# Moved keys copied once by ScalarE before the state increments read them, in a linear-attention and feed-forward kernel

## The chip, the cores and the metric

The kernel runs on 1 core of one Trainium2 chip. The metric is the device time of one execution in microseconds (us), and lower is better. TensorE (PE in the profile, with its weight loads as PEld) multiplies matrices, VectorE (DVE) and ScalarE (ACT) work elementwise, GpSimd (POOL) and SyncE (SP) here mostly issue DMA transfers. Each engine runs its own list of instructions in order.

## The reference, cut to what matters

```python
# q, k, v, f_logit: (B=4, H=8, S=768, D=48)
f = 1 / (1 + exp(-f_logit))
for t in range(S):
    state = f[:, :, t, :, None] * state + einsum('bhd,bhe->bhde', k[:, :, t], v[:, :, t])
    y[:, :, t] = einsum('bhd,bhde->bhe', q[:, :, t], state)
x = y.transpose(0, 2, 1, 3).reshape(B * S, H * D)      # 3072 x 384
h = x @ w_in                                           # 384 -> 2048
out = (max(h, 0) + alpha * min(h, 0)) @ w_out          # 2048 -> 384
```

The first half is a gated linear recurrence: a 48x48 state for each head decays by f and takes in the product of key and value. The second half is a feed-forward network with a leaky Relu. Everything is float32.

## The kernel before, in words

**Tiling.** The sequence is cut into 6 chunks of 128 positions and the batch into 2 pairs, which makes 12 steps, numbered 0 to 11 here; steps 0 and 1 are the first chunk (c = 0) of the two pairs. Inside a step all positions of a chunk are worked on at once by matrix products, and the state is carried to the next chunk of the same pair, in `vs[bp]`.

**Pieces and the hand-written order.** A step is a set of generators, each cut by `yield` into pieces. The letters in the lists START and USUAL (lines 31 to 40) call them: P `prepare` (loads, gates, decays, on ACT and DVE), K `keys_moved`, O `carry`, S and T `scores` of the two batch rows, Y `attend`, n `network` (of the step before, in the loop). `flat` writes the order out; every engine but POOL takes its instructions in exactly this order. Steps up to 4 are ordered by START, steps from 5 on by USUAL, which is repeated. A "+" there means a piece of the next step, so that the keys of step n are moved at the end of round n-1.

**How the keys travel.** The last part of `prepare` computes the decayed keys `ks`; line 415 transposes them in blocks of 32 on DVE into `kt`. `keys_moved` (lines 457 to 466) then puts the blocks in place with 16 DMAs from `kt` into `ksn`: 8 on SP's queue and 8 on POOL's. The third piece of `carry` reads them: line 532 multiplies keys and values to the state increments in the PSUM banks `pd`. Ahead of it, for every step with c > 0, line 525 issues two very small matmuls (64x64 by 64x4), one for each half of the partitions. Their result is never used: they read one column of each moved block, so that PE's waits for the 16 transfers stand on them. In steps 0 and 1 there is no transfer; there ACT copies transposed keys from PSUM (line 518). The fourth piece of `carry`, `moved(0)` (lines 542 to 546, DVE), adds the increments to the decayed state, and `attend` (line 623) needs it for the second half of the chunk. `moved(1)` follows in the last piece of `attend`.

**What stands around it.** From step 4 on PE does line 497 (products of the chunk's two halves, 32 records) just before line 525, and goes on with the network after line 532. ACT does the Relu of the network (`neg`, line 673), copies A (453, 504, 612), `us` (334) and `y` (630). `y` and `ksn` are the same buffer (one tag, one buffer). The network writes `ph` (line 668) into 4 PSUM banks in turn; a bank is free again when ACT has made `neg` and DVE both halves of `gate` (line 675, two instructions) of it. `neg` has two buffers, and after every fourth bank DVE makes four sums (line 754). The products `pa` to `pe` (line 707) use the same four banks.

Of the kernel before, what the change touches and what calls it, by code (L numbers as in the profile page):

```python
# [21 lines left out]
U = 2  # L22
# [16 lines left out]
)  # L39
USUAL = "S:2 T:2 n:3 P+ n S P+ T S n:3 T n Y n O P+ O P+ O Y n O P+ Y:2 n:2 P+:2 K+ n P+"  # L40

LOOSE = ("a", "w", "b", "g", "W", "i", "X")

def flat(start, usual, steps=12):
    out = []
    for word in start.split():
        key, _, times = word.partition(":")
        out += [(key,) if key in LOOSE else (key[0], int(key[1:]))] * int(times or 1)
    for n in range(BEGUN, steps + 1):
        for word in usual.split():  # L50
            key, _, times = word.partition(":")
            m = n + key.count("+") - (key == "n")
            if m < steps:
                out += [(key[0], m)] * int(times or 1)
    return out

ORDER = flat(START, USUAL)


@with_exitstack  # L60
def kernel(
# [30 lines left out]
    nc = tc.nc  # L92
# [3 lines left out]
    D = DM // H  # L96
# [3 lines left out]
    T = U * C  # L100
    W = U * HP * C
# [70 lines left out]
    for m in range(1, NB):  # L172
        lo = UO[m] + (4 if m == 1 else 0)
        n = NB - m
# [4 lines left out]
    for half in range(2):  # L179
        for m in range(1, NQ):  # L180
            n = NQ - m
# [9 lines left out]
    ident = const.tile([128, 128], F32, tag="ident", name="ident")  # L191
# [65 lines left out]
    def rows(par):  # L257
        return slice(64 * par, 64 * par + D)
# [4 lines left out]
    def halves(cc):  # L263

        return slice(CH * cc, CH * cc + CH), slice(CH * (1 - cc), CH * (1 - cc) + D)
# [191 lines left out]
    def keys_moved(bp, c, x):  # L457
# [7 lines left out]
                    in_=kt[32 * a:32 * (a + 1)].rearrange("p (g b x) -> p g b x", b=NJ, x=32)[:, :, b, 0:n])  # L465
        yield

    def carry(bp, c, x):

        i = f"{bp}_{c}"  # L470
        home = more if (bp, c) == steps[0] else pairs
        off = home[0]
        if not c:
            half = home[1]
            for u in range(U):
                for hp in range(HP):
                    for j in range(NJ):
                        g = (u * HP + hp) * NJ + j
                        o = (u * HP + hp) * 16
                        for par in range(2):  # L480
                            r_ = rows(par)
                            nc.tensor.matmul(half[DB * j:DB * (j + 1), par, o:o + 16], lhsT=x["k16"][r_, g],
                                             rhs=x["q16"][r_, g], start=True, stop=True)
            yield
            for u in range(U):
                o = u * HP * 16
                nc.scalar.copy(ad[:, u, :, :, 16:DB], half[:, :, o:o + HP * 16].rearrange("p r (h t) -> p r h t", h=HP))  # L487
            yield
        q3, ks, kh, f64 = (x[n] for n in ("q3", "ks", "kh", "f64"))
        for u in range(U):  # L490
            for hp in range(HP):
                a = (u * HP + hp) * NC2
                h_ = slice(64 * (hp % 2), 64 * (hp % 2) + 2 * DB)
                o = (u * HP + hp) // 2 * 2 * DB
                for par in range(2):
                    r_ = rows(par)
                    nc.tensor.matmul(off[h_, par, o:o + 2 * DB], lhsT=kh[r_, a:a + 2].rearrange("p c s -> p (c s)"),  # L497
                                     rhs=q3[r_, a:a + 2, 2], start=True, stop=True)
        yield
        for cc in range(NC2):  # L500
            s_ = slice(CH * cc, CH * cc + DB)
            for e in range(2):
                of = off[64 * e + DB * cc:64 * e + DB * (cc + 1), :, 0:U * HP * DB]
                nc.scalar.copy(A[s_].rearrange("p u (r h e) t -> p r u h e t", r=2, e=2)[:, :, :, :, e, CH * cc + DB:CH * (cc + 1)],
                               of.rearrange("p r (u h c t) -> p r u h c t", u=U, h=HP // 2, c=NC2)[:, :, :, :, cc])


        if not c:
            yield
            pk = home[1]  # L510
            for u in range(U):
                for hp in range(HP):
                    a = (u * HP + hp) * NC2
                    nc.tensor.transpose(pk[:, u, hp * 128:(hp + 1) * 128], ks[:, a:a + 2].rearrange("p c s t -> p (c s t)"), ident)
            yield
            ksn = x["ksn"] = work.tile([128, U, HP * 128], F32, tag="ksn", name=f"ksn_{i}", bufs=1)
            for u in range(U):
                nc.scalar.copy(ksn[:, u], pk[:, u])
        yield
        pd = home[1]  # L520
        ksn = x["ksn"]
        if c:
            for par in range(2):
                r_ = slice(64 * par, 64 * par + 64)
                nc.tensor.matmul(pd[r_, par, 508:512], lhsT=ident[r_, r_], rhs=ksn[r_, 0, 0:128:32], start=True, stop=True)  # L525
        for u in range(U):
            for hp in range(HP):
                for cc in range(NC2):
                    for par in range(2):
                        o = (u * HP + hp) * D  # L530
                        s_ = halves(cc)[0]
                        nc.tensor.matmul(pd[rows(par), cc, o:o + D],  # L532
                                         lhsT=ksn[s_, u, hp * 128 + 64 * par:hp * 128 + 64 * par + D],
                                         rhs=vs[bp][s_, cc, u, (2 * hp + par) * D:(2 * hp + par + 1) * D], start=True, stop=True)

        def moved(cc):

            of, to = halves(cc)[1], halves(1 - cc)[1]
            was, then = (vs[bp][p, a, :, 0:DM].rearrange("p u (h e) -> p u h e", e=D)
                         for p, a in ((of, cc), (to, 1 - cc)))  # L540
            if c or cc:
                nc.vector.tensor_tensor(then, was, f64[of].unsqueeze(3).broadcast_to((D, U, H, D)), ALU.mult)
            for par in range(2):
                now = pd[rows(par), cc, 0:U * HP * D].rearrange("p (u h e) -> p u h e", u=U, e=D)
                if c or cc:
                    nc.vector.tensor_tensor(then[:, :, par:H:2], then[:, :, par:H:2], now, ALU.add)
                else:
                    nc.scalar.copy(then[:, :, par:H:2], now)

        x["moved"] = moved  # L550
        yield
        moved(0)
        yield
# [236 lines left out]
    with tc.manual_schedule(engines={mybir.EngineType.PE, mybir.EngineType.DVE, mybir.EngineType.Activation,  # L790
                                     mybir.EngineType.SP}):
        run = {}
        for n, step in enumerate(steps):
            x = {}
            for key, stage_ in zip("POYKn", (prepare, carry, attend, keys_moved, network)):
                run[key, n] = stage_(*step, x)
            run["S", n], run["T", n] = (scores(u, *step, x) for u in range(U))
        for key in ORDER:
            next(run[key] if key in run else pieces[key[0]])
# [55 lines left out]
```

## Time and profile before

| | us |
|---|---|
| three runs | 610.0, 608.13, 609.3 |
| median | 609.3 |
| the profiled execution: its time | 608.89 |
| the profiled execution: its span, first to last instruction | 607.1 |
| granted TensorE clock, mean | 0.994 |

The span is what the profile's rows add up to; 1.8 us of the execution's time lie around it. PE is the busiest engine, DVE comes next. In the rows, a float32 matmul of the program is two records of PE (32 matmuls of line 532 are 64 records), "idle before" is the time in which the engine did nothing just before a row, with what ended it, and EVENT_SEMAPHORE is an instruction of an engine's queue that only waits.

### The profile page before, as it was taken

How to read it: one execution, taken by the hardware profiler on the slowest of the kernel's cores; microseconds unless marked ns; L12 is line 12 of the kernel's file. 1: busy time of each engine (PE TensorE's matmuls, PEld its weight loads, DVE VectorE, ACT ScalarE, POOL GpSimd, SP SyncE). 2: the span in 40 equal slices, each digit the busy share in tenths (PEclk: the TensorE clock that was granted, in tenths of full speed). 3: DMA queues.
4: the chain of work that ended last, by engine and by line, in shares of the span. 5: the costliest groups of instructions: out<-in, count | busy, mean ns of one | idle time of the engine just before them, and what ended most of it. 6: DMA issues, size and time to landing. Idle time of an engine off the chain costs nothing.

```text
span 607.1 us, 18178 instructions
## 1 busy us (share of the span) xinstructions
PE 583.9 (96%) x7786; PEld 521.8 (86%) x7786; DVE 495.0 (82%) x998; ACT 242.3 (40%) x419; POOL 85.4 (14%) x162
## 2 busy tenths in 40 slices
PE   4679999999999999999999999999999999999997
PEld 2568767899899899899899899899889899899997
DVE  7889999998997788598888988988988986982351
ACT  4579944424513712341550541542433424322110
POOL 9210014023003003003001201200300300300000
PEclk9979999999999999999999999999999999999999
DMA  8949516123033111402501601601601601201000
GB/s 269 312 148 350 186 37 141 36 77 92 11 94 99 19 27 36 149 2 56 155 2 46 165 3 42 169 3 41 171 1 39 170 4 29 53 2 24 30 1 26
DMA packets 52880, 50.36 MB, mean 83 GB/s; under 512 B 26720, under 2 KB 43360, under 8 KB 52800
## 3 DMA queue, kind: packets, MB, share of 16 engines
q1 hardware_dynamic: 42784, 37.46, 21.2%
q0 software_dynamic: 5504, 9.90, 6.4%
q10 hardware_dynamic: 4512, 1.85, 1.3%
q8 instruction: 61, 1.00, 0.7%
q14 instruction: 19, 0.16, 0.1%
HBM read 36.21 MB, written 4.72 MB: 67 GB/s over the span
## 4 chain that ended last, share of the span: by engine, by line
PE 92%; ACT 1%; issue 1%; DMA 1%; SPq 0%; DVE 0%; ACTq 0%; DVEq 0%
PE ph L668 42%; PE pa L707 10%; PE pc L707 9%; PE pair L569 6%; PE pe L707 5%; PE pd L707 4%; PE pb L707 4%; PE pair L623 4%; PE po L688 3%; PE pair L532 1%; PE pair L497 1%; DMA xT<-y 1%; PE pair L525 1%; PE xt L642 0%; ACT us L334 0%
## 5 line engine op out<-in xcount | busy, mean ns | idle before, releaser
L668 PE MATMUL ph<-xT,w_in_sb 128*128 128x256 f32 x1152 | 255.7, 381 | 0.0
L668 PEld LDWEIGHTS ph<-xT,w_in_sb 128*128 128x128 f32 x1152 | 216.7, 190 | 31.5 <-issue 1.4
L675 DVE SCALAR_TENSOR_TENSOR gate<-neg,om,ph 128x256 f32<-128x256 f32 x192 | 81.9, 479 | 40.0 <-ACT neg L673 39.8
L673 ACT ACTIVATE neg<-ph 128x512 f32<-128x512 f32 x96 | 56.3, 595 | 115.6 <-PE ph L668 76.9
L707 PE MATMUL pa<-w_out_sb,gate 128*128 128x192 f32 x352 | 61.9, 329 | 0.0
L707 PE MATMUL pc<-t,S 128*128 128x192 f32 x352 | 61.6, 328 | 0.0
L707 PEld LDWEIGHTS pa<-w_out_sb,gate 128*128 128x128 f32 x352 | 57.5, 190 | 1.3
L707 PEld LDWEIGHTS pc<-t,S 128*128 128x128 f32 x352 | 57.4, 190 | 0.4
L453 ACT COPY A<-q 48x512 f32<-48x512 f32 x44 | 27.1, 616 | 74.8 <-DVE q L401 74.4
L463 POOL DMA_DIRECT2D ksn<-kt x80 | 46.2, 586 | 73.2 <-DVE kt L415 46.6
L653 POOL DMA_DIRECT2D xT<-y x22 | 11.9, 545 | 302.5 <-ACT y L630 302.4
L588 DVE COPY_PREDICATED ad<-mquad,pair 128x224 f32<-128x224 int32 (+6 forms) x140 | 41.7, 298 | 5.8 <-PE pair L569 1.7
L578 DVE COPY_PREDICATED ad<-mraw,pair 128x256 f32<-128x256 int32 (+1 forms) x96 | 41.1, 452 | 4.3 <-ACT ad L487 1.3
L711 DVE SCALAR_TENSOR_TENSOR Csum<-pc,Csum 128x192 f32<-128x192 f32 x22 | 7.8, 356 | 39.9 <-PE pc L707 39.8
L357 DVE TENSOR_TENSOR us<-us,fs 128x768 f32<-128x768 f32 (+5 forms) x60 | 36.9, 615 | 1.1
L612 ACT COPY A<-ad 32x512 f32<-32x512 f32 x48 | 29.5, 615 | 20.4 <-DVE ad L588 19.8
L754 DVE TENSOR_TENSOR S<-gate 128x512 f32<-128x512 f32 x44 | 30.3, 688 | 0.8
L707 PE MATMUL pe<-w_out_sb,S 128*128 128x192 f32 x176 | 30.5, 327 | 0.0
L707 PE MATMUL pb<-t,gate 128*128 128x192 f32 x176 | 30.4, 326 | 0.0
L707 PE MATMUL pd<-w_out_sb,S 128*128 128x192 f32 x176 | 30.4, 326 | 0.0
L630 ACT COPY y<-pair 128x512 f32<-128x512 f32 x22 | 11.8, 589 | 46.4 <-PE pair L623 45.8
L707 PEld LDWEIGHTS pe<-w_out_sb,S 128*128 128x128 f32 x176 | 28.9, 190 | 0.1
(121 smaller groups left out, 740.6 us busy)
## 6 DMA issues: line engine op xcount, KB each, us to landing
w_out_raw<-in_w_out SPq DMA_DIRECT2D x8, 767.8 KB, 7.2
w_in_raw<-in_w_in SPq DMA_DIRECT2D x8, 767.2 KB, 10.4
out<-o SPq DMA_DIRECT2D x23, 192.0 KB, 2.0
q<-in_qT SPq DMA_DIRECT2D x8, 512.0 KB, 4.7
k<-in_kT SPq DMA_DIRECT2D x8, 512.0 KB, 5.9
f<-in_fT SPq DMA_DIRECT2D x7, 512.0 KB, 3.9
vs<-in_v SPq DMA_DIRECT2D x16, 192.0 KB, 6.4
ksn<-kt SPq DMA_DIRECT2D x80, 32.0 KB, 2.1
```

The lines of the kernel that those rows point to most:

```text
L357: nc.vector.tensor_tensor(us[:, :, UO[m]:UO[m] + 4 * n].rearrange("p g (i r) -> p g i r", r=4), us[:, :, skip:skip + 4 * n].rearrange("p g ...
L453: nc.scalar.copy(A[halves(cc)[1], :, par * HP:(par + 1) * HP, CH * cc:CH * (cc + 1)], q3[rows(par)].rearrange("p (u h c) s t -> p u h c (s ...
L463: (nc.gpsimd if a % 2 else nc.sync).dma_start(out=ksn[32 * b:32 * (b + 1)].rearrange("p u (h x) -> p (u h) x", h=HP)[:, :, 32 * a:32 * a + n],
L569: nc.tensor.matmul(to[DB * j:DB * (j + 1), par, hp * step + lo:hp * step + hi], lhsT=keys[r_, g * DB:(g + 1) * DB], rhs=by[r_, g, lo:hi], ...
L578: nc.vector.copy_predicated(adu[:, :, :, d:4], mraw[:, d, :, d:4].bitcast(I32).unsqueeze(1).broadcast_to((128, H, NB, n)), rv[:, :, QO[d]: ...
L588: nc.vector.copy_predicated(ad[:, u, :, :, 4 * m:DB], mquad[:, lo:lo + n].bitcast(I32).unsqueeze(1).unsqueeze(1).broadcast_to((128, 2, HP, ...
L612: nc.scalar.copy(A[s_].rearrange("p u h t -> p (u h) t")[:, :, s_], ad[s_].rearrange("p u r h t -> p (u r h) t"))
L668: nc.tensor.matmul(ph[:, j * T:(j + 1) * T], lhsT=w_in_sb[:, kt, m * 128:(m + 1) * 128], rhs=xT[:, kt], start=(kt == 0 and j == 0), stop=( ...
L673: nc.scalar.activation(neg, phv, AF.Relu, scale=-1.0)
L675: nc.vector.scalar_tensor_tensor(gate[:, m % NH, m // NH], neg[:, j], om[:, m:m + 1], phv[:, j], ALU.mult, ALU.add)
L707: nc.tensor.matmul(to[:, 0:DH], lhsT=of(f), rhs=by(f), start=(f == 0 and not more), stop=(f == NH - 1), skip_group_check=True)
L754: nc.vector.tensor_tensor(to, x_, y_, op)
```

## The change

A new generator, `landed` (letter M), copies the moved keys with ScalarE from `ksn` back into the buffer `kt` from which they were moved, 48 of every 64 columns, in one instruction of 128 partitions by 768 elements. The state increments of line 532 read this copy. The two small matmuls of line 525 are gone. M stands once in every step from 2 on: in START after the ninth network piece of step 1, the one with `pa` and `pb` (M2), and directly behind K3 and K4, and in USUAL at the head of the round. The order of everything else stays.

```diff
-O2:2 P3:2 n1 ... n2 K3 Y3 n2:3 O3 P4 O3 ... n3:3 K4 Y4 O4:3 P5:2
+M2 O2:2 P3:2 n1 ... n2 K3 M3 Y3 n2:3 O3 P4 O3 ... n3:3 K4 M4 Y4 O4:3 P5:2
...
-USUAL = "S:2 T:2 n:3 P+ n S P+ T S n:3 T n Y n O P+ O P+ O Y n O P+ Y:2 n:2 P+:2 K+ n P+"
+USUAL = "M S:2 T:2 n:3 P+ n S P+ T S n:3 T n Y n O P+ O P+ O Y n O P+ Y:2 n:2 P+:2 K+ n P+"
...
+    def landed(bp, c, x):
+        parts = "p u (g x) -> p (u g) x"
+        kn = x["kt"].rearrange("p (u y) -> p u y", u=U)
+        nc.scalar.copy(kn.rearrange(parts, x=64)[:, :, 0:D], x["ksn"].rearrange(parts, x=64)[:, :, 0:D])
+        x["ksn"] = kn
+        yield
...
         ksn = x["ksn"]
-        if c:
-            for par in range(2):
-                r_ = slice(64 * par, 64 * par + 64)
-                nc.tensor.matmul(pd[r_, par, 508:512], lhsT=ident[r_, r_], rhs=ksn[r_, 0, 0:128:32], start=True, stop=True)
         for u in range(U):
...
-            for key, stage_ in zip("POYKn", (prepare, carry, attend, keys_moved, network)):
+            for key, stage_ in zip("POYKMn", (prepare, carry, attend, keys_moved, landed, network)):
```

8 rows, old and new, of the table START are left out of this document.

## The prediction

> **What bounds the kernel now.** The page's busy times and the shares of its chain that ended last come first, then the chain in order of time.
>
> ```profile
> PE 583.9 (96%) x7786; PEld 521.8 (86%) x7786; DVE 495.0 (82%) x998; ACT 242.3 (40%) x419; POOL 85.4 (14%) x162
> ...
> PE 92%; ACT 1%; issue 1%; DMA 1%; SPq 0%; DVE 0%; ACTq 0%; DVEq 0%
> ```
>
> PE sets the end. What leaves PE's list, or makes PE wait, moves the time one for one; ACT has room on the average, so only the places matter where it is late. The guards of line 525 are looked at in the view of that line and in the chain (start, length, what).
>
> ```profile
> L525 PEldq EVENT_SEMAPHORE  x79: 51/51/51, 123.3 to 548.3; - x79
> ...
> 75.40 0.84 PE pair L569 x60
> 76.25 0.86 PE pair L532 x64
> ...
> 123.75 2.60 PE pb L707 x16
> ...
> 127.32 2.80 PE pc L707 x16
> ...
> 264.62 0.62 PE pair L497 x32
> ...
> 266.64 2.80 PE pc L707 x16
> ...
> 547.45 0.62 PE pair L497 x32
> 548.24 0.21 issue
> 548.63 0.81 PE pair L532 x62
> 549.45 2.80 PE pc L707 x16
> ```
>
> In step 1, without guards, line 532 follows its forerunner without a gap (75.40+0.84 = 76.24) and takes 0.86. In step 11 the stretch from line 497 to `pc` takes 549.45-547.45 = 2.00, where 0.62+0.86 = 1.48 is work: the guards cost 0.52. In step 5 it is 2.02, so 0.54; the rounds between repeat this. The guards' own matmuls are the smaller part: eight waits a step (79 in ten steps) of 51 ns are 0.41. In step 2 a long product stands ahead of the guards instead of line 497, and there 127.32-(123.75+2.60) = 0.97 is only 0.11 over 0.86: the waits ran beside the product.
>
> The Trainium skill ("TensorE: Matmul & The Clock Gate", section "Wait — 56ns, not 53.3ns?") states that small matmuls start no closer than about 25 ns apart. By that floor two guards are worth an estimated 0.05 a step and 0.5 in ten. By it the sum below would be +1.2+0.55-0.5 = +1.25 in place of -1.9. Step 2's 0.11 is near the floor, step 11's 0.52 is not, so the measured gap decides.
>
> **The change part by part.**
>
> *What goes.* Twenty guard matmuls and PE's 80 waits. In rounds 5 to 11 the copy is ready long before its reader (in round 5 at 245.5, worked out below, with line 497 at 264.62), and PE has by then waited for later work of ACT, so nothing replaces them: 7 x 0.52 = 3.6. In steps 2 and 3, 0.1 each.
>
> But DVE must follow. `attend` needs `moved(0)`, and DVE gets there behind `pc`:
>
> ```profile
> 493.26 0.87 DVE L675 SCALAR_TENSOR_TENSOR gate<-neg,om,ph 128x256 f32<-128x256 f32 x2 [1.77 <-ACT neg L673]
> ...
> 505.23 0.36 DVE L711 SCALAR_TENSOR_TENSOR Csum<-pc,Csum 128x192 f32<-128x192 f32 x1 [0.52 <-PE pc L707]
> ...
> 506.59 1.11 DVE L546 TENSOR_TENSOR vs<-vs,pair 48x384 f32<-48x384 f32 x2
> ...
> 507.65 2.17 PE L623 MATMUL pair<-A,vs 128*64 128x64 f32 x64
> ```
>
> `moved(0)` ends at 507.70 just as line 623 starts. DVE's only idle time between the gate at 493.26 and there is 0.52. It covers 0.52 of saving, no more; any lateness of DVE in this stretch is lost from the saving.
>
> *What comes.* One ACT copy of 768 elements a step, ten in all. No row has this size, so it is bounded:
>
> ```profile
> L630 ACT COPY y<-pair x22: 586/588/593, 89.7 to 557.5; 128x512 f32<-128x512 f32 x22
> L630 ACTq EVENT_SEMAPHORE  x77: 17/38/6253, 38.6 to 549.1; - x77
> ...
> 485.15 1.05 ACT L296 COPY qd<-q 128x1024 f32<-128x1024 f32 x1
> ```
>
> It lies between 0.59 and 1.05; I take the middle, 0.82. Sixteen waits come with it, but `y` stood behind the same sixteen (some eight instructions a step, 38 ns each), so they move from line 630 to the copy. After the last landing up to 0.5 of them can remain; I take 0.3.
>
> *Queues.* The copy waits for all 16 landings, and each Relu or copy behind it on ACT waits with it. SP and POOL issue the moves when the transpose is done, as before; the buffer `ksn` is free earlier, but the transpose is what they wait for. The next transpose into `kt` must now follow line 532, which DVE's `moved(0)` does already.
>
> *Rounds 6 to 11.* Rows of SP with the landing, of ACT and of DVE:
>
> ```profile
> L463 SPq DMA_DIRECT2D ksn<-kt x8: 606/612/884, 472.3 to 477.2; - x8
> ...
> DMA to landing us min/median/max: 1.8/2.0/2.5
> ...
> 476.76 2.50 ACT L453 COPY A<-q 48x512 f32<-48x512 f32 x4 [9.98 <-DVE q L401]
> 479.17 1.07 ACT L673 ACTIVATE neg<-ph 128x512 f32<-128x512 f32 x2
> ...
> 480.75 2.52 DVE L675 SCALAR_TENSOR_TENSOR gate<-neg,om,ph 128x256 f32<-128x256 f32 x6
> ```
>
> The last keys land at 477.2+2.0 = 479.2 to 479.7, when ACT has just ended line 453. The copy then runs from about 479.5 to 480.3 and the first `neg` ends at 480.9, not 479.8. DVE is busy until 480.75, so it is 0.2 to 0.8 late, and the 1.77 idle before 493.26 takes that up before the stretch that counts. Cost nothing; without this cover up to 0.8 a round.
>
> *Round 5* has the keys later:
>
> ```profile
> L463 SPq DMA_DIRECT2D ksn<-kt x8: 602/610/618, 237.9 to 242.4; - x8
> ...
> 248.79 10.63 PE L668 MATMUL ph<-xT,w_in_sb 128*128 128x256 f32 x48
> ```
>
> Landed at 244.4, copied by 245.5, first `neg` 246.1, first pair of gates 247.0. PE needs that bank at 248.79, a margin of 1.8. Cost nothing.
>
> *Step 4* puts the copy right before its reader. ACT first has a Relu:
>
> ```profile
> 204.71 0.60 ACT L673 ACTIVATE neg<-ph 128x512 f32<-128x512 f32 x1 [2.04 <-PE ph L668]
> ...
> 206.54 8.04 PE L668 MATMUL ph<-xT,w_in_sb 128*128 128x256 f32 x36
> ```
>
> The keys have landed. The copy runs from 205.31 to 206.13, line 532 can start at about 206.2 and ends at 207.1, where the network now goes on at 206.54: +0.55 (0.3 to 0.8 by the copy's bounds).
>
> *Step 3* puts it in the way of the Relus:
>
> ```profile
> L463 SPq DMA_DIRECT2D ksn<-kt x8: 586/610/1687, 147.1 to 153.1; - x8
> ...
> 153.81 1.24 ACT L612 COPY A<-ad 32x512 f32<-32x512 f32 x2
> ...
> 155.43 2.53 DVE L675 SCALAR_TENSOR_TENSOR gate<-neg,om,ph 128x256 f32<-128x256 f32 x6
> ...
> 177.56 0.36 DVE L711 SCALAR_TENSOR_TENSOR Csum<-pc,Csum 128x192 f32<-128x192 f32 x1 [0.65 <-PE pc L707]
> ...
> 178.92 1.12 DVE L546 TENSOR_TENSOR vs<-vs,pair 48x384 f32<-48x384 f32 x2
> ...
> 180.09 1.59 PE L569 MATMUL pair<-qd,k 48*32 48x80 f32 x128
> ```
>
> ACT would come to the copy at 153.8, but the last keys land at 153.1+2.0 = 155.1. With 0.3 of waits it runs from 155.4 to 156.2; line 612 ends at 157.5, the next `neg` at 158.1. The second of the three gate pairs at 155.43 would have run at 156.3: DVE is 1.8 late. From there to 177.56 I find no idle time in DVE's timeline; then 0.65 is taken up, and `moved(1)` ends not at 180.04 but 1.2 later. Line 569 writes the banks that it reads and starts 0.05 behind it: +1.2 for PE (0.9 to 1.6).
>
> *Sum.* -0.1 (step 2) +1.2 (step 3, whose own 0.1 is lost in the wait) +0.55 (step 4) -3.6 (rounds 5 to 11) = -1.9. Against the profiled execution's 608.89 that is 607.0. The median is 0.4 above that execution, so 607.4 on its scale.
>
> **The rivals.**
>
> *Step 3 costs nothing*, because the gates or `moved(1)` have slack that the timeline hides. For it: PE's product `pd` ends at about 180.04 too, so DVE need not have been the bound. Against: DVE's row is the later by its 0.05. Sum -0.1-0.1+0.55-3.6 = -3.2, so 606.1.
>
> *DVE takes the gain back* at `attend`: the 0.52 of cover and the 0.52 of saving are equal, and a copy late by one more us in rounds 5 to 10 could leave DVE late at 493.26. If half the saving goes in seven rounds, the sum is -0.1, so 609.2. Against: the 1.77 of idle time stands in between.
>
> *The gap stays, and the kernel is slower.* If the 0.5 is not the waits of the guards but what line 532 pays wherever it follows line 497's short matmuls, with the waits merely lying in it, rounds 5 to 11 save nothing and the two early costs remain: -0.1+1.2+0.55 = +1.65, so 611.0, and up to +2.3 with both at their upper ends. It decides at a leftover gap of 0.28 a round: above that the sum is positive. Against: the row of 76.25, and eight waits of 51 ns that fill 0.41 of the 0.52. This is also the case in which the change doesn't do what it says, freeing PE of the landings.
>
> **How the numbers follow.** Forecast 0.58 (own range 606.8 to 608.0, from steps 3 and 4 at their ends), step 3 free 0.16, DVE takes back 0.12, gap stays 0.14. The range goes from the second case with step 4 at +0.3 and rounds of 0.54 (605.6) to the third with step 4 at +0.8 (609.4); it leaves out the last. A measurement here tells about 0.3%, or 1.8 us, from no change. The forecast's -1.9 lies at that edge: half of it and the second case are faster, 0.45; the other half, the third case and half of the last are same, 0.48; the rest is slower, 0.07.
>
> **What would show it.** Right: no waits of PE at line 532 in rounds 5 to 11, and 1.48 from line 497 to `pc`; idle time of PE ahead of line 532 in step 4 (about 1.0, on the ACT copy) and ahead of line 569 in step 3 (1.2, on DVE line 546, by its new number); the new copy at 0.82. Wrong: idle time of PE at line 623 on DVE, or at line 668 on gates, in every round, or a copy near or above 1.05.

## The result and the profile after

| | before | changed |
|---|---|---|
| median of 20 runs, us | 610.08 | 606.54 |
| lowest to highest, us | 608.13 to 612.76 | 604.76 to 608.97 |
| ratio of the times, 95% interval | | 0.9944 (0.9930 to 0.9958) |
| profiled execution, us | 608.89 | 607.96 |
| its span, us | 607.1 | 606.2 |

The changed kernel is 3.4 us faster (2.6 to 4.3 by the interval). Behind the new generator its line numbers are higher: 497 is now 504, 532 is 535, 546 is 549, 569 is 572, 623 is 626, 673 and 675 are 676 and 678, 707 is 710.

The page first: busy time of the engines, and the shares of the chain.

```profile
PE 580.8 (96%) x7746; PEld 518.5 (86%) x7746; DVE 495.4 (82%) x998; ACT 248.5 (41%) x429; POOL 81.7 (13%) x162
...
PE 87%; DVE 5%; ACT 1%; DMA 1%; issue 1%; ACTq 0%; DVEq 0%
```

PE has 40 records less, the guards, and ACT ten instructions more, the copies. DVE's 5% of the chain are new (before it had 0%): somewhere PE now waits for it.

The chain in order of time (start, length, what), in step 2 and in round 10, answers to the guards' rows:

```profile
125.11 2.60 PE pb L710 x16
127.70 0.86 PE pair L535 x64
128.57 2.80 PE pc L710 x16
...
500.63 0.62 PE pair L504 x32
501.26 0.72 PE pair L535 x64
501.98 2.80 PE pc L710 x16
```

From line 504 to `pc` the stretch is 501.98-500.63 = 1.35, where it was 2.00. In step 2 the increments follow `pb` directly.

Next the rows of the copy itself, and the waits of PE's queue that are left at the increments:

```profile
L471 ACT COPY kt<-ksn x10: 831/832/834, 125.7 to 526.7; 128x768 f32<-128x768 f32 x10
...
L535 PEldq EVENT_SEMAPHORE  x4: 51/51/51, 27.1 to 207.4; - x4
```

Ten copies of 0.83 each; the last wait at line 535 is at 207.4, in step 4. None is left in rounds 5 to 11.

What was paid is read by stages. This view gives the start and end of each stage, its length, the busy time (and instructions) of PE, PEld, DVE, ACT and POOL in it, then granted clock, DMA share and GB/s. The cuts are the starts of the scores of step 2, step 4 and step 5 and of the last `pe`; the first fence is the kernel before, the second the changed one.

```profile
114.18:180.09 65.91, 65.86 (x850) 60.41 (x849) 61.45 (x120) 23.17 (x41) 9.41 (x16) 1.00 0.20 51
180.09:234.92 54.83, 54.63 (x677) 50.65 (x677) 45.15 (x92) 18.16 (x32) 9.64 (x17) 1.00 0.22 57
234.92:601.11 366.19, 364.68 (x4590) 334.90 (x4590) 283.08 (x593) 123.55 (x220) 35.98 (x64) 1.00 0.22 58
```

```profile
115.53:182.71 67.18, 66.19 (x842) 60.15 (x841) 61.88 (x121) 24.50 (x43) 9.38 (x16) 1.00 0.24 63
182.71:238.07 55.36, 54.40 (x672) 50.36 (x673) 45.19 (x92) 18.66 (x33) 9.91 (x18) 1.00 0.18 42
238.07:600.17 362.10, 362.09 (x4561) 332.45 (x4561) 283.62 (x593) 128.46 (x227) 35.62 (x63) 1.00 0.22 58
```

The rounds give 4.09, and the first two stages cost 1.27 and 0.53. In those two PE was idle (67.18 against 66.19 busy, 55.36 against 54.40), in the rounds not at all by this count. A longer row can still hide a wait: in round 5 the weight loads for `pe` stood 0.25 for ACT,

```profile
282.04 2.57 PEld L710 LDWEIGHTS pe<-w_out_sb,S 128*128 128x128 f32 x16 [0.25 <-ACT o L731]
```

and that round got only 0.4 shorter (47.15 to 46.76 between the scores of steps 5 and 6). The second profile of this kernel lost some 0.1 in the same round, e3, e4 and e5 nothing; ACT stood there behind its own issues of the `xT` transfers (3.78 where it was 2.88), and why was not tried.

The sum is -2.29. The start before the first cut took 1.35 more in this execution; among the ten profiles of this study it lies anywhere between 113.54 and 116.68, whatever the kernel, so it is left out of all sums below.

The waits themselves, in step 3 and step 4, as ACT, DVE and PE rows (idle time before a row and what ended it in brackets):

```profile
156.91 0.83 ACT L471 COPY kt<-ksn 128x768 f32<-128x768 f32 x1 [1.88 <-DMA ksn<-kt]
157.77 1.24 ACT L615 COPY A<-ad 32x512 f32<-32x512 f32 x2
...
159.66 1.66 DVE L678 SCALAR_TENSOR_TENSOR gate<-neg,om,ph 128x256 f32<-128x256 f32 x4 [2.11 <-ACT neg L676]
...
173.66 0.59 PE L710 MATMUL pa<-w_out_sb,gate 128*128 128x192 f32 x2 [0.19 <-DVE gate L678]
...
181.53 1.12 DVE L549 TENSOR_TENSOR vs<-vs,pair 48x384 f32<-48x384 f32 x2
...
182.71 1.59 PE L572 MATMUL pair<-qd,k 48*32 48x80 f32 x128 [0.65 <-DVE vs L549]
...
207.94 0.83 ACT L471 COPY kt<-ksn 128x768 f32<-128x768 f32 x1
...
208.82 0.94 PE L535 MATMUL pair<-vs,kt 64*48 64x48 f32 x64 [0.96 <-ACT kt L471]
```

One reads the chain downwards: ACT stands 1.88 for the landing, DVE 2.11 for the Relu behind the copy, PE at `pa` and again 0.65 at the scores, whose banks `moved(1)` reads until 182.65. In step 4 PE stands 0.96 for the copy.

### The profile page after: what moved, and what is told of

The parts are those of the page before. It is cut to its first block, busy times and chain, and to the rows that moved or that the text cites. A ratio compares the mean times of both kernels' runs of the same rounds, so it can differ in the third digit from the quotient of the medians.

```text
span 606.2 us, 18025 instructions
## 1 busy us (share of the span) xinstructions
PE 580.8 (96%) x7746; PEld 518.5 (86%) x7746; DVE 495.4 (82%) x998; ACT 248.5 (41%) x429; POOL 81.7 (13%) x162
## 4 chain that ended last, share of the span: by engine, by line
PE 87%; DVE 5%; ACT 1%; DMA 1%; issue 1%; ACTq 0%; DVEq 0%
PE ph L671 39%; PE pa L710 9%; PE pc L710 9%; PE pair L572 6%; PE pe L710 4%; PE pd L710 4%; PE pb L710 4%; PE pair L626 3%; PE po L691 3%; PE pair L535 1%; DVE gate L678 1%; PE pair L504 1%; DVE S L757 1%; DMA f<-in_fT 1%; PE xt L645 0%
## 5 line engine op out<-in xcount | busy, mean ns | idle before, releaser
L572 PEld LDWEIGHTS pair<-qd,k 48*32 48x32 f32 x1536 | 18.1, 111 | 13.6 <-ACT us L334 8.5
L572 PE MATMUL pair<-qd,k 48*32 48x80 f32 x1536 | 21.2, 248 | 8.5 <-DVE qd L303 7.8
```

Source lines behind the costliest of these rows:

```text
L572: nc.tensor.matmul(to[DB * j:DB * (j + 1), par, hp * step + lo:hp * step + hi], lhsT=keys[r_, g * DB:(g + 1) * DB], rhs=by[r_, g, lo:hi], ...
```

## The experiments

The theory: the price of the guards is PE's waits for the landings; the copy moves them to ACT, where they are free in rounds 5 to 11 and cost PE time in steps 3 and 4. The rivals: the guards' own matmuls are the price; the increments gain by reading another buffer; the copy's cost in steps 3 and 4 is chance. All ratios are to the kernel before, from runs on the same chip. The stages are those of above.

| kernel | step 2 to step 4 | step 4 to 5 | rounds 5 to 11 | sum against before | line 497/504 to `pc` in a round | ratio (95%) |
|---|---|---|---|---|---|---|
| before | 65.91 | 54.83 | 366.19 | | 1.99 to 2.02 | |
| before, again | 65.91 | 54.82 | 366.15 | -0.05 | 1.99 to 2.02 | |
| e1, guards gone | 65.70 | 54.83 | 365.89 | -0.51 | 1.91 to 2.00 | 0.9989 (0.9973 to 1.0004) |
| e2, copy unread | 67.20 | 54.88 | 366.15 | +1.30 | 1.99 to 2.02 | 1.0025 (1.0009 to 1.0042) |
| changed | 67.18 | 55.36 | 362.10 | -2.29 | 1.35 | 0.9944 (0.9930 to 0.9958) |
| changed, again | 67.42 | 55.45 | 361.91 | -2.15 | 1.34 to 1.35 | 0.9944 (0.9922 to 0.9965) |
| e6, guards on the copy | 67.27 | 55.47 | 362.36 | -1.83 | 1.45 | 0.9969 (0.9952 to 0.9985) |
| e3, copy of step 3 later | 65.70 | 55.37 | 361.76 | -4.10 | 1.34 to 1.35 | 0.9923 (0.9902 to 0.9944) |
| e4, copy of step 4 earlier | 67.32 | 54.41 | 361.84 | -3.36 | 1.34 to 1.35 | 0.9949 (0.9929 to 0.9970) |
| e5, both | 65.70 | 54.40 | 361.76 | -5.07 | 1.34 to 1.35 | 0.9912 (0.9890 to 0.9934) |

**e1: the guards taken out, nothing added.**

```diff
-        if c:
-            for par in range(2):
-                r_ = slice(64 * par, 64 * par + 64)
-                nc.tensor.matmul(pd[r_, par, 508:512], lhsT=ident[r_, r_], rhs=ksn[r_, 0, 0:128:32], start=True, stop=True)
```

> The guard matmuls are taken out and nothing else: no copy by ScalarE, the increments read the moved keys as before. Their first four matmuls now carry the 16 landings themselves. Theory (PE's waits are the price, some 0.4 us a round, the guards' matmuls the small rest): line 497 to pc in rounds 5 to 11 falls from 2.00 us only to 1.75 to 1.9, the whole by 0.7 to 1.7 us. Rival (the guards' matmuls themselves cost it): the stretch falls to 1.35 as in the changed kernel, and the whole by 4 us or more, since no copy costs anything in steps 3 and 4.

Measured: 1.91 to 2.00 in the rounds, the sum -0.5, and in the times no difference that the interval shows. The row of PE's queue at this kernel's line 528 (the increments) and its matmuls in round 10 (timeline):

```profile
L528 PEldq EVENT_SEMAPHORE  x81: 51/51/51, 26.3 to 548.7; - x81
```

```profile
500.48 0.69 PE L497 MATMUL pair<-q,kh 48*64 48x64 f32 x32
500.99 1.56 PE L528 MATMUL pair<-vs,ksn 64*48 64x48 f32 x64
502.48 0.76 PE L703 MATMUL pc<-t,S 128*128 128x192 f32 x3
```

The waits did not go with the guards, they moved into the increments, which now stretch over 1.56 (0.90 in the changed kernel's round 5). So the guards' matmuls were not the price. The expectation missed its numbers all the same: it had 1.75 to 1.9 for the stretch and 0.7 to 1.7 for the whole. Taking the waits at their 51 ns was too low, as is worked out further below.

**e6: the guards put back into the changed kernel, reading the copy.**

```diff
         ksn = x["ksn"]
+        if c:
+            for par in range(2):
+                r_ = slice(64 * par, 64 * par + 64)
+                nc.tensor.matmul(pd[r_, par, 508:512], lhsT=ident[r_, r_], rhs=ksn[r_, 0, 0:128:32], start=True, stop=True)
```

> The changed kernel with the two guard matmuls put back, but reading the copy, so that they are issued without any wait for a landing. Theory (the waits were the price): line 504 to pc in rounds 5 to 11 is 1.40 to 1.50 us, the whole 0.4 to 1 us slower than the changed kernel. Rival (the guards' matmuls were the price): 1.9 to 2.0 us, and the whole 4 us slower than the changed kernel.

The timeline of this kernel's round 10 has the guards (line 532 here) between line 504 and the increments (line 539):

```profile
502.02 0.69 PE L504 MATMUL pair<-q,kh 48*64 48x64 f32 x32
502.53 0.17 PE L532 MATMUL pair<-kt,ident 64*64 64x4 f32 x1
...
502.62 0.92 PE L539 MATMUL pair<-vs,kt 64*48 64x48 f32 x62
503.47 1.73 PE L714 MATMUL pc<-t,S 128*128 128x192 f32 x9
```

503.47-502.02 = 1.45. Guards without waits cost 0.10 a round in this stretch, so of the 0.65 that the change takes from it 0.55 go with the waits. The stages of the whole are 0.3 to 0.5 longer than in the two profiles of the changed kernel, at the lower end of the expected 0.4 to 1. Theory held for the stretch. The other buffer is not the gain either: with no wait ahead of them the increments take 0.86 from `ksn` in step 1 (76.25 in the prediction's chain) and 0.86 from the copy in step 2 of the changed kernel (127.70 above).

**e2: the copy made, but read by nobody.** Against the changed kernel:

```diff
-        x["ksn"] = kn
...
+        if c:
+            for par in range(2):
...
```

(the guards are back, on the moved keys, and the increments read those)

> The copy is added in all ten places, but the guards stay and the increments go on reading the moved keys, so the copy is read by nobody. Theory: step 3 pays its 1.2 to 1.5 us (ScalarE's Relus late, VectorE late, PE idle ahead of the scores of step 4), step 4 pays nothing since PE does not wait for the copy, rounds 5 to 11 stay at 2.00 us from line 497 to pc: 1.2 to 1.6 us slower than before. Rival (ScalarE's copy is hidden everywhere, and what the changed kernel's profile shows in step 3 is chance): no difference from before.

Measured: the first stage +1.29, the second +0.05, the rounds as before; 1.5 us slower by the ratio (0.5 to 2.6). ACT and PE in step 3 of this kernel:

```profile
154.95 0.83 ACT L471 COPY kt<-ksn 128x768 f32<-128x768 f32 x1 [1.80 <-DMA ksn<-kt]
```

```profile
180.74 1.59 PE L575 MATMUL pair<-qd,k 48*32 48x80 f32 x128 [0.66 <-DVE vs L552]
```

The same wait as in the changed kernel, with nobody reading the copy: step 3 is paid by ACT's place in the order alone, and step 4's 0.53 comes from PE's wait for the copy. In the seven rounds the copy costs nothing.

**e3: the copy of step 3 two Relus later.**

```diff
-... n2 K3 M3 Y3 n2:3 O3 P4 O3 ...
+... n2 K3 Y3 n2:2 M3 n2 O3 P4 O3 ...
```

> The changed kernel with the copy of step 3 two Relus later (behind the network pieces that it held up, still ahead of its reader). Theory: PE's idle time ahead of the scores of step 4 (0.65 us, and 0.19 us plus slower progress in pa) goes, 1.2 to 1.5 us less than the changed kernel, a ratio of about 0.992 to before. Rival (that stretch is not set by the copy): same as the changed kernel, 0.9944.

ACT in step 3, and the two PE rows around the scores:

```profile
154.72 0.60 ACT L676 ACTIVATE neg<-ph 128x512 f32<-128x512 f32 x1
156.06 0.60 ACT L676 ACTIVATE neg<-ph 128x512 f32<-128x512 f32 x1 [0.74 <-DVE gate L678]
156.68 0.83 ACT L471 COPY kt<-ksn 128x768 f32<-128x768 f32 x1
```

```profile
176.82 2.76 PE L710 MATMUL pd<-w_out_sb,S 128*128 128x192 f32 x16
179.63 1.59 PE L572 MATMUL pair<-qd,k 48*32 48x80 f32 x128
```

The copy no longer waits, nor does PE: the stage is 65.70, 1.48 under the changed kernel and 0.21 under before. Theory held.

**e4: the copy of step 4 one Relu earlier.**

```diff
-... n3:3 K4 M4 Y4 O4:3 ...
+... n3:2 K4 M4 n3 Y4 O4:3 ...
```

> The changed kernel with the copy of step 4 one Relu earlier, so that it is done when the increments come. Theory: PE's 0.96 us of idle time ahead of the increments of step 4 goes, 0.9 to 1.1 us less than the changed kernel (its 0.53 over before, and the guards' 0.5 that a step without idle time saves), a ratio of about 0.9928. Rival (the keys land too late, the copy then holds up the Relu behind it): the idle time moves to a bank of the network, same as the changed kernel.

ACT and PE in step 4:

```profile
204.30 0.83 ACT L471 COPY kt<-ksn 128x768 f32<-128x768 f32 x1 [0.63 <-DMA ksn<-kt]
205.72 0.60 ACT L676 ACTIVATE neg<-ph 128x512 f32<-128x512 f32 x1 [0.58 <-PE ph L671]
```

```profile
205.56 0.69 PE L504 MATMUL pair<-q,kh 48*64 48x64 f32 x32
206.08 0.90 PE L535 MATMUL pair<-vs,kt 64*48 64x48 f32 x64
```

The copy fits before the Relu, which waits for PE anyway. The stage falls to 54.41, 0.95 under the changed kernel's. The times don't show it: the expected ratio of 0.9928 did not come, and 0.9949 beside 0.9944, with intervals 0.3 to 0.4% wide, are too coarse for 1 us. So here the stage is the evidence.

**e5: both shifts.**

> The changed kernel with both shifts: the copy of step 3 two Relus later and the copy of step 4 one Relu earlier. The stages were independent so far, so both gains should add: from the scores of step 2 to those of step 4 65.7 us in place of 67.2, step 4 54.4 in place of 55.4, the rounds as they are; about 5 us under before, a ratio near 0.992. Rival (taking both waits away leaves another engine in the way): no better than the one with the later copy of step 3 alone, 0.9923.

The stages of this kernel (length, then busy time of PE, PEld, DVE, ACT, POOL):

```profile
116.21:181.91 65.70, 65.66 (x842) 60.24 (x841) 61.87 (x120) 24.44 (x43) 9.37 (x16) 1.00 0.23 61
181.91:236.31 54.40, 54.40 (x673) 50.39 (x673) 45.16 (x92) 18.76 (x33) 9.91 (x18) 1.00 0.20 46
236.31:598.07 361.76, 361.76 (x4561) 332.73 (x4561) 283.36 (x593) 128.49 (x227) 35.56 (x63) 1.00 0.23 58
```

Both gains add. PE is busy through all three stages; the kernel is 0.9912 of before (0.9890 to 0.9934), the fastest here, and its sum of -5.07 agrees with the times. Against e3 alone (0.9923) the times can't tell it apart.

**e7 and e8: the changed kernel and the one before once more.**

> The changed kernel once more. The first profile's stages add up to -2.3 us without the start, the times to -3.4 (-2.6 to -4.3). Theory: step 3 costs 1.2 to 1.5 us in every execution and the rounds give 0.6 each, so that the stages again add up to -2.3 to -2.7, and the ratio lies nearer 0.996. Rival (step 3's cost depends on when the keys happen to land): less than 0.8 in step 3 here.

> The kernel before, for a second profile. Theory: the time up to the scores of step 2 (114.18 us in the first) differs by about a microsecond either way, as it does among the kernels that are the same up to there, and all later stages repeat within 0.1 us.

The stages repeat: before within 0.04, the changed one within 0.24. Step 3 costs 1.27 and 1.51 with what steps 2 and 3 save already taken off, and 1.29 to 1.41 in e2, e4 and e6, where its copy stands in the same place, so it is no chance. The sum of -2.15 falls just short of the expected -2.3 to -2.7. The expected ratio near 0.996 did not come either: it is 0.9944 again (0.9922 to 0.9965), though the medians of these few runs, 607.06 and 609.59, are only 2.5 apart. The stage sums of -2.15 and -2.29 lie inside this interval, but a little outside that of the 20 runs (-2.6 to -4.3). Of e1, e2, e3, e4, e5 and e6 the sums lie in their intervals. In all ten profiles the time is the start and the three stages plus 7.8, so what the stages don't hold, a microsecond or so of the changed kernel's gain, would lie in the start, which varies by 3 us between profiles. Whether the change or chance put it there was not settled.

## Why the prediction was right in sign and short in size

The forecast was 607.4 where the median was 609.3, so -1.9. By the stages the change is worth -2.29 and -2.15, with each cost in the step where it was forecast; by the ratio of the times it is 3.4, which would be 605.9 on that scale, inside the range. Of the 1.5 between forecast and times, the stages explain 0.4 at most; the rest is the microsecond that stays open.

- **Rounds 5 to 11.** Forecast -3.6, measured -4.1 to -4.4 in the kernels that have the change as it is or shifted. The mis-sized term is the work left in the stretch: 1.48 was forecast, 1.35 measured. The 0.86 for line 532 was taken from step 1, and in step 2 of the changed kernel it is 0.86 too, behind `pb`. Behind line 504 it is 0.72. In the timeline of the changed kernel's round 5 the increments start while line 504 still runs:

```profile
267.72 0.69 PE L504 MATMUL pair<-q,kh 48*64 48x64 f32 x32
268.24 0.90 PE L535 MATMUL pair<-vs,kt 64*48 64x48 f32 x64
```

  268.24 is 0.17 before 267.72+0.69. Line 497 and the first guard of round 10 before overlapped by only 0.07 (500.26+0.69 against 500.88). What lets the groups overlap was not tried apart, and it is not all: in e1 the increments start 0.18 before line 497 ends (500.48+0.69-500.99), and the stretch still stays near 2.

  The other small term is the wait, put at 51 ns, 0.41 for eight. The view of the guards' line in round 10 before has all eight of a step:

```profile
L525 PEldq EVENT_SEMAPHORE  x8: 51/51/51, 500.4 to 501.2; - x8
```

  Seven steps from 500.4 to 501.2 are 0.11 each, about twice the 51 ns that a wait reads. Some run beside line 497, which ends at 500.95; three start behind that end. In step 2 they start from 123.3 on, beside `pa` and `pb`, and cost next to nothing, as the prediction read it. How the 0.55 divides between the spacing of the waits and the lost overlap stays open. The guards' own matmuls, an estimated 0.05 a step in the prediction, measured 0.10 (e6).
- **DVE at `attend`.** Forecast: it covers 0.52 of saving and no more. The cover is used up, as the chain of DVE and PE in the changed kernel's round 5 shows:

```profile
271.43 0.77 DVE L341 TENSOR_TENSOR_SCAN ss<-fs,ones 128x289 f32<-128x289 f32 x1
272.08 0.37 DVE L714 SCALAR_TENSOR_TENSOR Csum<-pc,Csum 128x192 f32<-128x192 f32 x1
...
273.45 1.11 DVE L549 TENSOR_TENSOR vs<-vs,pair 48x384 f32<-48x384 f32 x2
...
274.47 2.22 PE L626 MATMUL pair<-A,vs 128*64 128x64 f32 x64
```

  The idle time ahead of `Csum` (0.54 in this round before) is gone, and line 626 takes 2.22 in place of 2.17. So a round gets some 0.6 of the 0.65: between the scores of steps 7 and 8, for example, it is 46.56 where it was 47.14, and in e3 every round is 0.61 to 0.66 shorter. The limit of 0.52 was a tenth too low. `Csum` starts 0.65 behind the scan of line 341 here (272.08-271.43), where it was 1.28 before (269.55-268.27): DVE could come 0.63 earlier, since its rows overlap a little where it does not wait.
- **Step 2.** Forecast -0.1 there and in step 3. In e3 and e5, where nothing waits, the stage is 0.21 shorter: right. It is the same in e1, so here it is the guards' matmuls.
- **Step 3.** Forecast +1.2, measured +1.27 and +1.51 for the stage, with step 2's gain inside it. The mechanism was the forecast one (landing, Relu, gates, `moved(1)`, scores), and e3 removes it whole. Its place was half wrong: PE already loses time in `pa`, where it reads gates (3.57 from 170.52 to `pb` at 174.09, where it was 2.70 before), and only 0.65 at the scores. The forecast put all of it at the scores.
- **Step 4.** Forecast +0.55, measured +0.53 and +0.62.
- **The copy.** Forecast 0.82 between bounds of 0.59 and 1.05, measured 0.83. In round 5 it ended later than forecast and still cost nothing:

```profile
248.29 0.83 ACT L471 COPY kt<-ksn 128x768 f32<-128x768 f32 x1 [7.44 <-DMA ksn<-kt]
...
249.65 3.27 DVE L678 SCALAR_TENSOR_TENSOR gate<-neg,om,ph 128x256 f32<-128x256 f32 x8 [5.79 <-ACT neg L676]
...
251.97 10.63 PE L671 MATMUL ph<-xT,w_in_sb 128*128 128x256 f32 x48
```

  The first pair of gates is done at about 250.5, PE needs the bank at 251.97: the margin is 1.5, where 1.8 was forecast.
- **The rivals.** "Step 3 costs nothing" and "the gap stays" are refuted, by e2 and by the 1.35. "DVE takes the gain back" is real by some 0.05 a round (line 626), not by half.

## What to carry to other kernels

A matmul that only stands in for PE's waits costs mostly what the waits cost, here 0.55 us a round for sixteen transfers: without it the waits move to the next reader (e1), but one instruction of an engine with idle time, placed early, can take them all. The price is then paid wherever this instruction stands in its engine's order before its data has landed, or just before its reader; so each place is to be checked against the landing, and in this kernel shifting two of ten places was worth another 2.8 us by the stages. The idle time of the next engine says roughly how much of such a gain can be kept: DVE's 0.52 a round in the forecast, 0.6 in the runs.

## What the runs showed of the hardware

Eight waits of PE's queue read 51 ns each but start 0.11 us apart (500.4 to 501.2, kernel before), and with them 0.55 of the stretch went, beside the guards' own 0.10 (e6). Line 504 and the increments ran into each other by 0.17 us where no wait stood between them (changed kernel), against 0.07 for line 497 and a guard with waits. The copy of 128x768 from `ksn` to `kt` by ScalarE took 831 to 834 ns in all ten places, between 588 ns for the 512 elements of line 630 and 1.05 us for the 1024 of line 296.
